# Remainder tokens of a recurrence-and-FFN kernel: from 128 partitions by batch to 96 partitions with two tokens of every batch

## The chip, the cores and the metric

The kernel runs on one core of a Trainium2 chip. Times are device microseconds. Before the change the median of three runs is 236.07 us (235.56 to 237.6). One further execution was profiled; all views of the trace are of that one.

## The reference

For a batch of 4 sequences of 6,336 tokens with 256 channels, a gated recurrence runs along the tokens, and a highway layer follows on every token:

```python
sig = 1.0 / (1.0 + np.exp(-f_logit))
f = lower_bound + (1.0 - lower_bound) * sig
i = 1.0 - f
for t in range(S):
    h = f[:, t] * h + i[:, t] * x[:, t]
    y[:, t] = h
H = np.maximum(y @ w_h, 0.0)
T = 1.0 / (1.0 + np.exp(-(y @ w_t + b_t)))
out = T * H + (1.0 - T) * y
```

Inputs and output are 32-bit floats in HBM, 26 MB each for `x`, `f_logit` and the output.

## The kernel before, in words

The 25,344 tokens are cut into 29 units (the table `UNITS`): mostly 1,024 tokens of one batch, some of 512 or 256 at both ends, and one, unit 15, of 768 tokens: the 192 tokens from 3,072 on of each of the four batches, which 1,024 does not divide. A row of the table holds the tokens per partition (k), the runs (batch, first token, count), the column at which the product e is split between VectorE and GpSimd, and how the tokens of a partition are grouped for the product B, for the output matmuls O and for the stores o.

Each unit goes through the same steps, which the code names by a letter:

- `l`, `x`: loads of `f_logit` and `x` by SyncE (L223). A partition takes k consecutive tokens. For one batch `in_dram` (L212) gives the access "p j d"; for unit 15 it gives "b p j d", so that the batch (4 steps) is the outer step, and partitions 32b to 32b+31 hold 6 tokens each of batch b.
- `U`: ScalarE's sigmoid of the negated logits (L259), giving u, the part that does not gate.
- `B`: the product bv = u * x (L281 on GpSimd; L279 on VectorE for units 0 and 1).
- `T`, `V`: TensorE's transposes of u and bv to channels by tokens (L287, L305), for each half h of the channels.
- `F`: ScalarE makes the gate f = 1 + ncc * u from the transposed u, and puts the tokens in order (L297).
- `S`: VectorE's scan along the tokens (L313), with the state carried per batch and half. Unit 15 has eight scans of 192.
- `Z`, `G`: the two matmuls of the layer (L324); `A`: ScalarE's sigmoid t (L335); `D`: VectorE's maximum d (L339); `E`, `P`: the product e = d * t on VectorE (L345) and, for the columns past the split, on GpSimd (L352).
- `O`: TensorE sums y and e back into token rows, in groups of two tokens per partition (L363, L364); `C`: ScalarE copies them out of PSUM (L376); `o`: SyncE stores them (L381).

The order of all the work is written out in one list, `OPS`. It is also the order in which each engine issues its own part, and it names the buffer of each result (`l15@l2` is the load of unit 15's logits into slot l2; there are four slots each for l and x, eight for o). All loads and stores stand in one queue, SyncE's: a load that waits for its slot, or a store that waits for its copy, holds everything behind it. The list was made by a planner outside the kernel. `X` items are matmuls on zeros.

In the list before, the part of SyncE around unit 15 reads: `l14 o6.0 x17 o7.0 o5.0 x14 l15 x15 o8.1 o4.0 o8.0 l16 o5.1 x16 o9.0 x18`, and later `o10.0 o15.1 o15.0 x24 l23 l26`.

Of the kernel before, what the change touches and what calls it, by code (L numbers as in the profile page):

```python
# [36 lines left out]
    (6, ((0, 3072, 192), (1, 3072, 192), (2, 3072, 192), (3, 3072, 192)), 384, (4, 2), (2, 2, 2), (4, 2), ()),  # L37
# [23 lines left out]
X4@s0 Tb@s0 cst l0@l0 x0@x0 W1 W0 U0.0@u0 B0.0@bv0 X1@s1 T0.0@s1 T0.1@s2 F0.1@f0 F0.0@f1 w1 l1@l1 U1.0@u1  # L61
V0.0@s3 V0.1@s0 dia v1 S0.0@y0 X7@s2 T1.0@s2 S0.1 w0 v0 l2@l2 x1@x1 F1.0@f2 U2.0@u2 T1.1@s1 X3@pp0 Z0.0@pp0
X1@s3 T2.0@s3 F1.1@f3 A0.0@t0 B1.0@bv1 V1.1@s2 S1.1@y1 T2.1@s0 G0.0@pp1 Z0.1@pp0 V1.0@s1 D0.0@d0 X1@pp1
G0.1@pp1 S1.0 F2.0@f1 F2.1@f0 A0.1 x2@x2 B2.0@bv2 l3@l3 l4@l0 U3.0@u0 x3@x3 l5@l1 B3.0@bv0 X1@pp0 Z1.1@pp0
D0.1 A1.1@t1 U4.0@u1 G1.1@pp1 D1.1@d1 V2.0@s3 T3.1@s2 T3.0@s0 Z1.0@pp0 G1.0@pp1 S2.0@y2 F3.1@f3 F3.0@f2
V2.1@s1 S2.1 X1@s3 T4.1@s3 T4.0@s2 F4.1@f1 A1.0 F4.0@f0 D1.0 E1@e0 E0@e1 X4@pp1 G2.0@pp1 D2.0@d1 x4@x0 x5@x1
l6@l2 U5.0@u2 V3.0@s0 Z2.1@pp0 V3.1@s1 O0.0@s3 Z2.0@pp1 S3.0@y3 S3.1 A2.1@t1 A2.0 T5.1@s2 T5.0@s0 G2.1@pp0
C0.0@o0 F5.1@f2 D2.1 B4.0@bv1 B5.1@bv2 B5.0 Z3.0@pp1 V4.0@s1 O1.0@s3 Z3.1@pp0 V4.1@s2 A3.0@t0 F5.0@f3 A3.1
U6.0@u0 G3.1@pp1 G3.0@pp0 C1.0@o1 S4.0@y4 S4.1 D3.1@d0 D3.0 E2@e1 E3@e0 x6@x2 l8@l3 l7@l0 x7@x3 x8@x0 o0.0
o1.0 l9@l1 x9@x1 Z4.0@pp1 V5.0@s1 T6.0@s0 S5.0@y0 A4.0@t1 F6.0@f0 B6.0@bv0 B6.1 Z4.1@pp0 A4.1 O2.0@s2 O3.1@s3  # L70
C3.1@o2 U8.0@u1 C2.0@o3 V5.1@s0 G4.1@pp1 T6.1@s3 G4.0@pp0 S5.1 D4.0@d1 D4.1 V6.0@s1 U7.0@u2 F6.1@f1 Z5.0@pp0
T8.1@s0 V6.1@s2 Z5.1@pp1 S6.0@y1 B7.1@bv1 B7.0 A5.0@t0 F8.1@f3 A5.1 O3.0@s3 G5.1@pp0 T7.1@s1 S6.1 D5.1@d0
T7.0@s0 G5.0@pp1 E4@e0 D5.0 F7.1@f2 C3.0 F7.0@f0 Z6.1@pp0 V7.0@s2 A6.1@t1 U9.0@u0 O2.1@s1 O4.1@s3 V7.1@s0
Z6.0@pp1 B8.0@bv2 B8.1 S7.0@y3 S7.1 E5@e1 A6.0 T8.0@s2 G6.1@pp0 G6.0@pp1 T9.0@s0 C2.1 C4.1@o4 F8.0@f1 F9.0@f0
O4.0@s1 V8.1@s3 O5.2@s2 C4.0 C5.2@o5 l13@l2 l10@l3 U10.0@u2 x10@x2 l11@l0 D6.0@d1 D6.1 B9.1@bv0 B9.0 S8.1@y2
E6@e0 G7.1@pp1 T9.1@s0 O5.1@s1 Z7.0@pp0 D7.1@d0 T10.1@s2 V8.0@s3 C5.1@o6 F9.1@f2 A7.0@t0 F10.1@f3 O5.0@s1 C5.0
U11.0@u1 V9.0@s0 G7.0@pp0 Z7.1@pp1 O6.1@s2 C6.1@o7 x11@x3 o3.0 l12@l1 l17@l3 x12@x0 x13@x1 o2.0 S8.0 B10.0@bv1
B10.1 B11.1@bv2 O5.3@s1 D7.0 T11.0@s3 V9.1@s2 A7.1 P7.0@e1 B11.0 Z8.1@pp0 F11.0@f1 C5.3 A8.1@t1 S9.0@y4 S9.1
Z8.0@pp1 O6.3@s3 O6.2@s1 A8.0 T10.0@s0 G8.1@pp0 G8.0@pp1 O6.0@s2 C6.3@o0 U13.0@u0 C6.2 C6.0 F10.0@f0 D8.1@d1
D8.0 E7 E8@e0 V10.1@s3 Z9.0@pp0 S10.1@y0 O7.3@s1 A9.0@t0 C7.3@o1 T11.1@s2 F11.1@f2 V10.0@s0 G9.1@pp1 O7.0@s1  # L80
C7.0@o2 D9.1@d0 U12.0@u2 Z9.1@pp0 O7.2@s3 C7.2 S10.0 V11.0@s2 G9.0@pp1 V11.1@s1 O7.1@s3 T13.0@s0 A9.1 C7.1
F13.0@f3 Z10.1@pp0 D9.0 P8.0 B13.0@bv0 B13.1 B12.1@bv1 P9.0@e1 B12.0 T12.0@s3 G10.0@pp1 O8.2@s0 A10.1@t1
Z10.0@pp0 F12.0@f0 C8.2@o3 A10.0 l14@l0 o6.0 x17@x2 o7.0 o5.0 x14@x3 l15@l2 O8.3@s3 C8.3 x15@x1 o8.1 o4.0
S11.0@y1 D10.0@d1 S11.1 O8.1@s2 O8.0@s0 C8.1@o7 C8.0 U14.0@u1 G10.1@pp1 T13.1@s3 G11.1@pp0 T12.1@s2 D10.1 E9
E10@e0 D11.1@d0 V12.0@s1 Z11.0@pp1 O9.3@s0 S12.0@y3 F12.1@f1 F13.1@f2 A11.0@t0 C9.3@o2 Z11.1@pp0 O9.0@s2
V12.1@s3 S12.1 C9.0@o6 A11.1 B14.1@bv2 P10.0 B14.0 U15.0@u0 V13.0@s0 O9.2@s1 C9.2 O9.1@s2 G11.0@pp1 C9.1
U17.0@u2 G12.0@pp0 T14.1@s3 V13.1@s1 o8.0 l16@l1 o5.1 x16@x0 o9.0 x18@x3 l19@l0 D11.0 D12.0@d1 B15.0@bv1
P11.0@e1 S13.1@y2 S13.0 E11 Z12.1@pp1 G12.1@pp0 F14.1@f0 T15.1@s2 T14.0@s3 O10.3@s1 A12.1@t1 Z12.0@pp1
F14.0@f1 C10.3@o3 V14.0@s3 O10.1@s1 O10.2@s0 A12.0 Z13.1@pp1 C10.1@o4 F15.1@f2 A13.1@t0 C10.2 O11.2@s1
O10.0@s2 D12.1 S14.0@y4 B17.1@bv0 B15.1 P12.0@e0 G13.1@pp0 D13.1@d0 C11.2@o7 C10.0 U16.0@u1 O11.3@s0 T15.0@s1  # L90
V14.1@s3 C11.3 O11.0@s2 F15.0@f3 C11.0@o5 Z13.0@pp1 G13.0@pp0 O11.1@s0 A13.0 B16.1@bv2 S14.1 D13.0 E12 E13@e1
P13.0 B16.0 B17.0 T16.0@s1 T17.1@s3 V15.0@s2 C11.1 F16.0@f1 F17.1@f0 o9.1 l18@l2 o7.1 o6.1 l24@l3 o11.1 l20@l1
x19@x1 o10.1 S15.0@y0 Z14.1@pp0 Z14.0@pp1 O12.3@s0 V15.1@s1 O12.0@s3 T17.0@s2 A14.1@t1 C12.3@o6 A14.0 S15.1
G14.1@pp0 O12.1@s0 G14.0@pp1 D14.1@d1 D14.0 O12.2@s1 C12.0@o2 U18.0@u0 C12.2 C12.1 F17.0@f3 G15.1@pp0 V16.0@s3
P14.0@e0 D15.1@d0 S16.0@y1 E14 Z15.1@pp1 O13.2@s1 C13.2@o1 T16.1@s0 F16.1@f2 O13.0@s2 Z15.0@pp0 V16.1@s1
C13.0@o0 A15.1@t0 A15.0 V17.0@s0 O14.0@s3 C14.0@o7 S16.1 G15.0@pp1 O13.3@s2 O14.2@s3 O13.1@s1 D15.0 U19.0@u2
C13.3 B18.0@bv1 B18.1 P15.0@e1 B19.1@bv2 S17.0@y3 C13.1 C14.2@o3 Z16.0@pp0 G16.0@pp1 A16.0@t1 T18.0@s2
V17.1@s1 T18.1@s3 O14.1@s0 D16.0@d1 S17.1 F18.0@f1 G16.1@pp0 Z16.1@pp1 F18.1@f2 C14.1 A16.1 V18.0@s2 T19.1@s3
T19.0@s0 O14.3@s1 F19.1@f3 C14.3 F19.0@f0 D16.1 E15 E16@e0 S18.0@y2 P16.0 B19.0 Z17.0@pp1 V18.1@s3 O15.1@s1
G17.1@pp0 O15.0@s0 o12.1 l22@l2 o13.0 o11.0 x20@x0 l21@l0 o12.0 o14.1 x23@x2 x22@x3 x21@x1 o10.0 D17.1@d0  # L100
S18.1 A17.0@t0 C15.1@o6 U20.0@u1 C15.0 G17.0@pp1 O16.0@s2 C16.0@o0 Z17.1@pp0 A17.1 D17.0 T20.1@s1 O16.2@s0
O15.2@s2 V19.0@s3 B20.0@bv0 B20.1 P17.0@e1 Z18.0@pp0 C16.2@o5 C15.2@o2 F20.1@f1 A18.0@t1 G18.0@pp1 O16.3@s0
C16.3 O16.1@s2 V19.1@s1 S19.0@y4 D18.0@d1 S19.1 E17 U21.0@u0 Z18.1@pp0 V20.1@s3 T20.0@s0 G18.1@pp1 A18.1 C16.1
F20.0@f2 Z19.0@pp0 D18.1 S20.1@y0 B21.1@bv1 B21.0 P18.0@e0 A19.0@t0 O17.0@s1 T21.1@s2 F21.1@f0 U22.0@u2
V20.0@s0 G19.0@pp1 D19.0@d0 S20.0 G19.1@pp0 C17.0@o3 T21.0@s2 O17.3@s3 C17.3@o4 Z19.1@pp1 F21.0@f3 T22.1@s1
O17.1@s3 O17.2@s2 V21.1@s0 A19.1 D19.1 E18 E19@e1 o15.1 o15.0 x24@x0 l23@l1 l26@l0 C17.2 o17.1 o16.1 o16.0
S21.1@y1 Z20.1@pp1 C17.1 F22.1@f1 V21.0@s2 O18.1@s3 Z20.0@pp0 A20.1@t1 C18.1@o2 A20.0 S21.0 U23.0@u1 B22.0@bv2
P19.0 G20.0@pp1 O18.0@s1 O18.2@s3 G20.1@pp0 T22.0@s0 O18.3@s2 C18.0 C18.2@o6 C18.3 B22.1 D20.0@d1 D20.1
O19.2@s1 G21.1@pp1 U24.0@u0 F22.0@f2 C19.2@o4 D21.1@d0 B23.1@bv0 P20.0@e0 B23.0 x25@x1 l25@l2 o14.0 x26@x3
l28@l1 o17.0 o18.1 o13.1 o18.0 l27@l3 T23.0@s3 V22.1@s2 Z21.0@pp0 G21.0@pp1 V22.0@s0 A21.0@t0 S22.1@y3 S22.0  # L110
F23.0@f0 T24.0@s1 O19.3@s2 Z21.1@pp0 F24.0@f3 O19.1@s3 O19.0@s1 T23.1@s0 D21.0 A21.1 G22.0@pp0 C19.0@o5 C19.3
C19.1 F23.1@f1 E20 V23.0@s1 O20.2@s2 C20.2@o0 T24.1@s3 F24.1@f2 E21@e1 D22.0@d1 Z22.0@pp1 Z22.1@pp0 V23.1@s0
S23.0@y2 S23.1 B24.0@bv1 P21.0 B24.1 A22.0@t1 A22.1 O20.0@s2 C20.0@o7 U25.0@u2 O20.3@s3 G22.1@pp1 O21.0@s1
O21.3@s2 C21.3@o3 C21.0@o6 C20.3 G23.1@pp0 D22.1 D23.1@d0 B25.1@bv2 B25.0 O20.1@s0 V24.1@s2 T25.0@s1 C20.1
U26.0@u1 G23.0@pp1 V24.0@s3 T25.1@s0 P22.0@e0 S24.1@y4 D23.0 S24.0 E22 Z23.0@pp0 O21.2@s2 F25.1@f0 F25.0@f1
Z23.1@pp1 C21.2 V25.0@s0 O21.1@s1 V25.1@s2 A23.0@t0 A23.1 B26.1@bv0 B26.0 P23.0@e1 S25.1@y0 Z24.0@pp0 C21.1
U27.0@u0 A24.0@t1 G24.1@pp1 T26.1@s3 O22.2@s1 T26.0@s2 C22.2@o1 F26.0@f2 F26.1@f3 D24.1@d1 S25.0 Z24.1@pp0
T27.0@s1 G24.0@pp1 O22.3@s2 O22.1@s3 O22.0@s0 A24.1 C22.3 C22.1@o2 C22.0 F27.0@f0 Z25.0@pp0 V26.1@s2 D24.0 E23
E24@e0 x28@x2 x27@x0 o19.1 o19.0 o20.1 o20.0 o21.0 o22.0 o21.1 O23.2@s3 O23.0@s0 O23.3@s1 G25.0@pp1 A25.0@t0
C23.2@o4 C23.3 C23.0@o5 o23.1 o22.1 O23.1@s3 T27.1@s1 V26.0@s0 U28.0@u2 Z25.1@pp0 F27.1@f1 C23.1 S26.1@y1  # L120
P24.0 B27.0@bv1 B28.0@bv2 D25.0@d0 S26.0 A25.1 T28.1@s2 G25.1@pp1 T28.0@s1 O24.3@s3 G26.0@pp0 D25.1 D26.0@d1
# [10 lines left out]
def kernel(  # L132
# [66 lines left out]

    def need(key, n):  # L200
        if key not in st[n]:
            k = UNITS[n][0]
            shape, dt = {
                "l": ([P, 8, D], FP32), "x": ([P, 8, D], FP32), "u": ([P, 8, D], FP16), "bv": ([P, 4, D, 2], BF16),
                "f0": ([P, 8 * P], FP16), "f1": ([P, 8 * P], FP16), "y": ([P, NH, 8 * P], BF16),
# [222 lines left out]
```

## Time and profile before

| | |
|---|---|
| median of the runs | 236.07 us |
| profiled execution, its own time | 238.39 us |
| its span | 236.6 us |
| granted TensorE clock, mean | 0.962 |
| busy: PE, DVE, ACT, POOL | 201.3, 197.5, 201.0, 151.2 us |
| moved by DMA | 78.68 MB, 333 GB/s over the span |
| loads of 1,024 KB: issue to landing, median | 15.8 us (l), 14.8 us (x) |
| loads of 768 KB (unit 15) | one of l, one of x |
| ACT waited for l | 16.1 us in 4 waits, longest 9.5 |
| POOL waited for x | 38.3 us in 9 waits, longest 16.1 |
| SyncE's queue waited for ACT's copies | 78.0 us in 26 waits, longest 7.8 |

The profile names engines PE (TensorE), DVE (VectorE), ACT (ScalarE), POOL (GpSimd) and SP (SyncE). The page cuts the span in 40 slices of 5.9 us and gives the busy share of each engine in tenths; slices are counted from 0. A busy-time line gives a stretch, and for each engine the busy microseconds and the number of instructions, then the granted clock, the mean busy share of the 16 DMA engines, and GB/s.

### The profile page before, as it was taken

The page shows a single profiled execution, that of the slowest core. Times are in us where ns is not written, and L with a number is a line of the kernel's source. Part 1 is how long each engine was busy: PE and PEld are TensorE (multiplying, and loading weights), DVE is VectorE, ACT ScalarE, POOL GpSimd, SP SyncE. Part 2 cuts the span into 40 slices and gives each one's busy share as a digit, 9 for nine tenths or more (in the row PEclk, how much of TensorE's full clock was granted, in tenths as well). Part 3 has the DMA queues.
Part 4 walks back from the last instruction along what each step waited for, and adds up shares of the span by engine and source line. Part 5 has one row for each costly group of instructions (what it writes and reads, how often), then busy time and mean ns, then how long its engine had stood idle before and what let it go on. Part 6 is the DMA issues. An engine that isn't in the chain of part 4 may idle for free.

```text
span 236.6 us, 4629 instructions
## 1 busy us (share of the span) xinstructions
PE 201.3 (85%) x1818; PEld 141.1 (60%) x1818; DVE 197.5 (83%) x163; ACT 201.0 (85%) x248; POOL 151.2 (64%) x80
## 2 busy tenths in 40 slices
PE   7779889899999980688986969999949999999991
PEld 3356556576677660366664756766636777686771
DVE  3488999999999990394996988999946999999970
ACT  5799999999999940959949879999667999998892
POOL 2066568579889680049698637919887299878400
PEclk9999999999999998589999999999976999999999
DMA  6999999999999999559999599989999949547286
GB/s 210 350 423 421 417 414 421 418 420 419 419 418 334 382 208 232 180 171 332 425 425 377 208 346 345 425 320 427 375 341 416 375 179 346 222 159 288 107 336 269
DMA packets 16221, 78.68 MB, mean 333 GB/s; under 512 B 1732, under 2 KB 2248, under 8 KB 10824
## 3 DMA queue, kind: packets, MB, share of 16 engines
q1 hardware_dynamic: 16192, 78.39, 86.8%
q8 instruction: 14, 0.23, 0.4%
q14 instruction: 7, 0.06, 0.1%
q10 hardware_dynamic: 8, 0.00, 0.0%
HBM read 52.43 MB, written 25.95 MB: 331 GB/s over the span
## 4 chain that ended last, share of the span: by engine, by line
DMA 34%; PE 33%; DVE 19%; issue 6%; SPq 2%; POOL 2%; ACT 1%; ACTq 0%; DVEq 0%; POOLq 0%
DMA out_dram<-o 25%; DVE y L313 11%; DMA l<-in_f_logit_dram 9%; PE gp L324 8%; PE zp L324 8%; DVE d L339 7%; PE op L364 5%; PE op L363 4%; PE bT L305 4%; PE uT L287 4%; SPq L223 2%; DVE e L345 2%; ACT o L376 1%; POOL e L352 1%; POOL bv L281 1%
## 5 line engine op out<-in xcount | busy, mean ns | idle before, releaser
L281 POOL TENSOR_TENSOR bv<-u,x 128x1024 bf16<-128x1024 f16 (+1 forms) x49 | 103.9, 2138 | 58.6 <-DMA x<-in_x_dram 38.3
L313 DVE TENSOR_TENSOR_SCAN y<-f,y,bT 128x1024 bf16<-128x1024 f16 (+3 forms) x56 | 103.8, 1878 | 13.6 <-ACT o L376 9.1
L339 DVE SCALAR_TENSOR_TENSOR d<-y,ncc,gp 128x1024 bf16<-128x1024 bf16 (+3 forms) x58 | 63.6, 1112 | 11.1 <-PE gp L324 6.4
L376 ACT COPY o<-op 128x512 f32<-128x512 f32 x99 | 59.0, 651 | 6.9 <-DMA out_dram<-o 4.9
L259 ACT ACTIVATE u<-l 128x2048 f16<-128x2048 f32 (+3 forms) x29 | 49.9, 1721 | 16.2 <-DMA l<-in_f_logit_dram 16.1
L335 ACT ACTIVATE t<-zp,bt 128x1024 bf16<-128x1024 f32 (+3 forms) x58 | 60.4, 1056 | 3.2 <-issue 1.7
L363 PE MATMUL op<-diag,y 128*128 128x128 f16 x396 | 56.8, 224 | 6.6 <-ACT o L376 5.5
L297 ACT ACTIVATE f<-uT,ncc 128x1024 f16<-128x1024 f16 (+3 forms) x58 | 59.3, 1050 | 3.0 <-PE uT L287 3.0
L324 PEld LDWEIGHTS <-w_sb 128*128 128x128 f16 x408 | 38.5, 100 | 35.5 <-issue 10.5
L364 PE MATMUL op<-ident_b,e 128*128 128x128 bf16 x396 | 56.8, 226 | 2.0 <-DVE e L345 1.1
L364 PEld LDWEIGHTS <-e 128*128 128x128 bf16 x396 | 49.7, 142 | 13.0 <-issue 9.1
L352 POOL TENSOR_TENSOR e<-d,t 128x1152 bf16<-128x1152 bf16 (+1 forms) x20 | 46.9, 2345 | 14.6 <-DVE e L345 9.3
L324 PE MATMUL gp<-y,w_sb 128*128 128x512 bf16 (+1 forms) x204 | 53.3, 382 | 1.7 <-ACT t L335 0.9
L324 PE MATMUL zp<-y,w_sb 128*128 128x512 bf16 (+1 forms) x204 | 53.1, 380 | 1.4 <-ACT t L335 0.5
L363 PEld LDWEIGHTS <-y 128*128 128x128 bf16 x396 | 51.3, 143 | 4.5
L305 PE MATMUL bT<-ident_f,bv 128*128 128x128 f32 x198 | 32.9, 284 | 10.5 <-ACT o L376 9.1
L287 PE MATMUL uT<-ident_h,u 128*128 128x128 f16 x396 | 31.4, 224 | 5.5 <-ACT o L376 1.8
L287 PEld LDWEIGHTS <-u 128*128 128x128 f16 x396 | 26.6, 101 | 14.9 <-issue 5.1
L305 PEld LDWEIGHTS bT<-ident_f,bv 128*128 128x128 f32 x198 | 23.4, 145 | 17.3 <-ACT o L376 9.8
L345 DVE TENSOR_TENSOR e<-d,t 128x896 bf16<-128x896 bf16 (+4 forms) x29 | 21.2, 752 | 1.7 <-PE op L364 1.0
L313 DVE TENSOR_TENSOR_SCAN y<-f,bT 128x1024 bf16<-128x1024 f16 (+2 forms) x8 | 12.5, 1604 | 0.0
L386 PE MATMUL zeros<-zeros 128*128 128x512 bf16 x23 | 8.3, 471 | 2.7 <-DVE zeros L174 1.2
(25 smaller groups left out, 11.8 us busy)
## 6 DMA issues: line engine op xcount, KB each, us to landing
out_dram<-o SPq DMA_DIRECT2D x48, 512.0 KB, 10.0
l<-in_f_logit_dram SPq DMA_DIRECT2D x21, 1024.0 KB, 15.8
x<-in_x_dram SPq DMA_DIRECT2D x21, 1024.0 KB, 14.8
l<-in_f_logit_dram SPq DMA_DIRECT2D x5, 512.0 KB, 10.6
x<-in_x_dram SPq DMA_DIRECT2D x5, 512.0 KB, 9.0
out_dram<-o SPq DMA_DIRECT2D x3, 256.0 KB, 13.2
l<-in_f_logit_dram SPq DMA_DIRECT2D x1, 768.0 KB
x<-in_x_dram SPq DMA_DIRECT2D x1, 768.0 KB
```

What stands on the lines that cost most here:

```text
L259: pin(nc.scalar.activation(need("u", n)[:, :k], st[n]["l"][:, :k], AF.Sigmoid, scale=-1.0))
L281: on_pool(pin(nc.gpsimd.tensor_mul(o, u, v)))
L287: pin(nc.tensor.transpose(t[:, j * P:(j + 1) * P], st[n]["u"][:, j, h * P:(h + 1) * P], ident_h))
L297: pin(nc.scalar.activation(a, b, AF.Identity, scale=ncc[:, h:h + 1], bias=1.0))
L305: pin(nc.tensor.transpose(w[:, g], v[:, g, h * P:(h + 1) * P, 0], ident_f))
L313: pin(nc.vector.tensor_tensor_scan(y[:, h, c:c + m], st[n][f"f{h}"][:, c:c + m], st[n]["bT", h][:, c:c + m], 0.0 if prev is None else prev ...
L324: pin(nc.tensor.matmul(p[:, a:e], w_sb[:, k, ki, m * P:(m + 1) * P], st[n]["y"][:, ki, a:e], start=ki == 0, stop=ki == NH - 1))
L335: pin(nc.scalar.activation(need("t", n)[:, m, :N], st[n]["zp", m][:, :N], AF.Sigmoid, bias=bt[:, m:m + 1]))
L339: pin(nc.vector.scalar_tensor_tensor(need("d", n)[:, m, :N], st[n]["y"][:, m, :N], ncc[:, m:m + 1], st[n]["gp", m][:, :N], op0=ALU.mult, o ...
L363: pin(nc.tensor.matmul(o, st[n]["y"][:, h, j:k * P:k], diag[:, h], start=True, stop=False))
L364: pin(nc.tensor.matmul(o, st[n]["e"][:, h, j:k * P:k], ident_b, start=False, stop=True))
L376: pin(nc.scalar.copy(st[n]["o", s][:, j0 - base:j1 - base].rearrange("p j d -> p (j d)"), st[n]["op", q][:, :(j1 - j0) * D]))
```

## The change

Unit 15 takes 96 partitions and 8 tokens in each: two consecutive tokens of each of the four batches. A copy of it between HBM and SBUF now has the partition as its outer step on both sides ("p b j d"), with pieces of two tokens (2,048 bytes). Its transposes, products and output matmuls are sized by 96 rows, and the tokens are put in order by batch in `F`, `V` and `O`. Its groups are those of the 1,024-token units: two products B of 4, four output groups of 2, two stores of 4 tokens per partition; the split of e is at column 448 instead of 384. The other units compute as before. The list `OPS` is made anew from end to end: the same items, but for unit 15's, in another order with other buffers, with 24 matmuls on zeros instead of 23.

```diff
-    (6, ((0, 3072, 192), (1, 3072, 192), (2, 3072, 192), (3, 3072, 192)), 384, (4, 2), (2, 2, 2), (4, 2), ()),
+    (8, ((0, 3072, 192), (1, 3072, 192), (2, 3072, 192), (3, 3072, 192)), 448, (4, 4), (2, 2, 2, 2), (4, 4), ()),
...
-    def in_dram(ap, n):
-        k, runs = UNITS[n][:2]
-        (b, a, m), q = runs[0], len(runs)
-        if q == 1:
-            return ap[b, a:a + m, :].rearrange("(p j) d -> p j d", j=k)
-        assert [(r, a, m) for r in range(b, b + q)] == list(runs)
-        return ap[b:b + q, a:a + m, :].rearrange("b (p j) d -> b p j d", j=k)
+    def shape(n):
+        k, runs = UNITS[n][:2]
+        r = len(runs)
+        b, a, m = runs[0]
+        assert [(b + i, a, m) for i in range(r)] == list(runs) and m * r % k == 0
+        return m * r // k, k, r, k // r, m * r
+
+    def copy(n, tile_, dram, to_dram=False, j0=0, j1=None):
+        np_, k, r, kr, _ = shape(n)
+        j1 = k if j1 is None else j1
+        b, a, m = UNITS[n][1][0]
+        t = tile_[:np_, :j1 - j0]
+        if r == 1:
+            d = dram[b, a:a + m, :].rearrange("(p j) d -> p j d", j=kr)[:, j0:j1]
+        else:
+            d = dram[b + j0 // kr:b + j1 // kr, a:a + m, :].rearrange("b (p j) d -> p b j d", j=kr)
+            t = t.rearrange("p (b j) d -> p b j d", j=kr)
+        pin(nc.sync.dma_start(d, t) if to_dram else nc.sync.dma_start(t, d))
...
-            pin(nc.tensor.transpose(t[:, j * P:(j + 1) * P], st[n]["u"][:, j, h * P:(h + 1) * P], ident_h))
+            pin(nc.tensor.transpose(t[:, j * np_:(j + 1) * np_], st[n]["u"][:np_, j, h * P:(h + 1) * P], ident_h[:np_, :np_]))
...
+            a = f[:, :N].rearrange("c (b p j) -> c b p j", b=r, j=kr)
+            b = st[n]["uT", h][:, :N].rearrange("c (b j p) -> c b p j", b=r, j=kr)
...
+            b, i = divmod(j, kr)
+            cols = slice(b * np_ * kr + i, (b + 1) * np_ * kr, kr)
...
-                pin(nc.tensor.matmul(o, st[n]["y"][:, h, j:k * P:k], diag[:, h], start=True, stop=False))
+                pin(nc.tensor.matmul(o, st[n]["y"][:, h, cols], diag[:, h], start=True, stop=False))
```

The first lines of the two lists, and SyncE's order around unit 15:

```diff
-X4@s0 Tb@s0 cst l0@l0 x0@x0 W1 W0 U0.0@u0 B0.0@bv0 X1@s1 T0.0@s1 T0.1@s2 F0.1@f0 F0.0@f1 w1 l1@l1 U1.0@u1
-V0.0@s3 V0.1@s0 dia v1 S0.0@y0 X7@s2 T1.0@s2 S0.1 w0 v0 l2@l2 x1@x1 F1.0@f2 U2.0@u2 T1.1@s1 X3@pp0 Z0.0@pp0
+l1@l0 X4@s0 Tb@s0 l0@l1 cst dia U1@u0 x0@x0 U0@u1 X3@s1 T0.1@s1 T1.0@s2 T0.0@s3 F0.1@f0 F0.0@f1 F1.0@f2
+B0.0@bv0 V0.1@s0 S0.1@y0 V0.0@s1 S0.0 W1 W0 w0 w1 v0 v1 X8@pp0 Z0.0@pp0 l2@l2 x1@x1 U2@u2 A0.0@t0 Z0.1@pp1
...
-l14 o6.0 x17 o7.0 o5.0 x14 l15 x15 o8.1 o4.0 o8.0 l16 o5.1 x16 o9.0 x18
+l16 o3.0 o6.1 x16 o7.1 o5.1 l15 x15 x17 o6.0 x19 o9.0 o9.1 l18 o7.0 o10.0 l19
...
-x21 o10.0 o15.1 o15.0 x24 l23 l26
+x23 o15.0 l23 o16.0 x24 l25 o16.1 x25 o17.1 l27 o18.0 x28 o14.0 l26 o18.1 o15.1
```

## The prediction

> **What bounds the kernel now.** I read the page's slices first, to see where all engines stop; then busy time by stretch, which separates the undisturbed part from the disturbed one; then the timelines of ScalarE and SyncE at the worst place; then the landing times of the stores issued there.
>
> ```profile
> PE 201.3 (85%) x1818; PEld 141.1 (60%) x1818; DVE 197.5 (83%) x163; ACT 201.0 (85%) x248; POOL 151.2 (64%) x80
> PE   7779889899999980688986969999949999999991
> DVE  3488999999999990394996988999946999999970
> ACT  5799999999999940959949879999667999998892
> GB/s 210 350 423 421 417 414 421 418 420 419 419 418 334 382 208 232 180 171 332 425 425 377 208 346 345 425 320 427 375 341 416 375 179 346 222 159 288 107 336 269
> ```
>
> One slice is 5.9 us. Two engines, ACT and DVE, are each busy about 200 of 236.6 us, and both are full until slice 13. At slice 15 (89 to 95 us) every engine stands at 0 or near it, while the moved bytes fall from 420 to about 200 GB/s over four slices. A second, smaller hole is at slices 29 and 30.
>
> The busy time by stretch (busy us of each engine, granted clock, share of the 16 DMA engines, GB/s):
>
> ```profile
> 12.00:84.00 72.00, 65.51 (x597) 45.45 (x595) 69.85 (x57) 71.29 (x84) 54.74 (x26) 1.00 1.00 405
> 24.00:84.00 60.00, 55.20 (x508) 38.50 (x506) 59.65 (x43) 60.00 (x68) 46.38 (x23) 1.00 0.99 402
> 84.00:108.00 24.00, 13.70 (x99) 8.91 (x99) 13.52 (x9) 11.75 (x13) 7.88 (x4) 0.79 0.77 210
> 100.00:104.00 4.00, 4.00 (x30) 2.63 (x28) 4.00 (x4) 2.35 (x3) 0.32 (x1) 0.68 0.25 104
> 84.00:192.00 108.00, 87.51 (x790) 62.38 (x791) 85.64 (x63) 84.23 (x99) 68.07 (x32) 0.92 0.91 329
> 192.00:228.00 36.00, 35.72 (x350) 26.50 (x349) 35.48 (x29) 33.86 (x48) 26.77 (x13) 1.00 0.58 224
> ```
>
> From 24 to 84 us ACT (fourth engine column) never stops and DVE (third) stops for 0.35 us: there the two compute engines bound the kernel, with the DMA just keeping up. From 84 to 192 DVE stands for 22.4 us and ACT for 23.8. The line for 100 to 104 us shows what kind of hold it is: the DMA share is 0.25 and 104 GB/s move, a quarter of 420. A quarter of 16 engines is four, and unit 15's transfers are the only ones whose outer step counts four (the batches).
>
> What ACT and the SyncE queue did there:
>
> ```profile
> 84.19 1.30 ACT L335 ACTIVATE t<-zp,bt 128x1024 bf16<-128x1024 f32 x1
> 94.97 1.48 ACT L259 ACTIVATE u<-l 128x1536 f16<-128x1536 f32 x1 [9.48 <-DMA l<-in_f_logit_dram]
> ```
> ```profile
> 74.44 1.15 SPq L223 DMA_DIRECT2D l<-in_f_logit_dram  x1
> 75.70 0.58 SPq L223 DMA_DIRECT2D x<-in_x_dram  x1
> 77.73 3.24 SPq L381 DMA_DIRECT2D out_dram<-o  x3
> ```
>
> The 128x1536 activation is unit 15's sigmoid; it waits 9.48 us for the load issued at 74.44. Of stores issued from 77.5 to 87 us, and from 40 to 75, the landing times are:
>
> ```profile
> DMA to landing us min/median/max: 26.9/27.7/28.4
> ```
> ```profile
> DMA to landing us min/median/max: 4.9/7.5/17.3
> ```
>
> Ordinary stores behind unit 15's two loads land 27.7 us after issue, where 7.5 was the median before: every transfer needs all engines, so each waits for the four clogged ones.
>
> **The change, part by part.**
>
> *Loads of unit 15.* Each is 768 x 1,024 B = 0.786 MB. Both at the shown 104 GB/s need 15.1 us; at the 420 GB/s of slices 2 to 11 they need 3.7. Now the outer step is 96 rows, of four pieces of 2,048 B each. No row shows 96; the nearest are the 128-row transfers at 420 GB/s, and the four-row ones at 104. So the two cost 3.7 to 15.1 us of the stream; 96 is near 128, so I take 3.7.
>
> *Stores of unit 15.* 0.786 MB together: 7.6 us on four engines, 1.9 on all. Behind these stores (issued around 152 us) stand the loads of units 23, 24 and 26, and the hole at slices 29 and 30 follows.
>
> [...]
>
> *Compute of unit 15*, from the rows by shape. ACT: the sigmoid becomes 2,048 long (1,973 ns for 1,482, +0.5) and there is one more eviction of 128x512 (651 ns, +0.65): +1.1 us. DVE: the product e takes 896 columns (767 ns for 551): +0.2; the eight scans of 192 stay (582 ns). POOL: the second bv product grows from 512 to 1,024 (2,158 for 1,170 ns), e shrinks by a sixth: +0.7, hidden, since POOL is 24% idle from 12 to 84 us. PE: 8 more matmuls in the output step, 4 and 2 more transposes, 14 in all at some 0.06 to 0.11 us spacing: about 1 us, hidden in PE's 9% idle there. ACT and DVE have no cover. That operations on 96 partitions cost the same by length is assumed; their cost lies between the same and three quarters of it.
>
> *The new list.* All issue orders change, with the same operations (one more zeros matmul, 24 for 23, about 0.2 us of PE's idle start). Head: S0 now stands ahead of the weight folds v0 and v1, for which DVE waited 1.70 us; l0 stands behind l1, 256 KB, some 0.9 us at the 283 GB/s of the first 12 us. So between -1.7 and +0.9. I take 0, because DVE's next product waits for x1 anyway (till 10.52 us), and the same bytes stand ahead of x1 as before. Tail: the last units are the same; the 228 to 236.6 stretch keeps its cost, within about 1 us. Middle: in the new order of SyncE, 25 loads stand directly behind a store, 18 before; l15 itself is behind two stores, the first of which waits for C7.3. From C7.3 to U15 ACT has about 14 us of work and a 1 MB load lands a median 15.8 us after issue, so a wait of about 2 us can arise there.
>
> *The sum.* In 84 to 192 us DVE has 85.64 us of work, plus 0.2. At the undisturbed rate of 12 to 84 (69.85 of 72, 97.0%) that takes 88.5 us instead of 108: 19.5 saved. By ACT: 84.23 + 1.1 at 71.29 of 72 takes 86.2: 21.8 saved. The engine that ends later decides: 19.5. This leaves about 2.7 us for stalls of the new order, which covers the possible 2 us at U15. PE ran at a granted clock of 0.50 around 96 to 102 us, after the standstill; that goes with it. The span becomes 236.6 - 19.5 = 217.1. The profiled execution took 238.39, 1.8 around its span; so 218.9. It stands 2.3 above the median of the runs (236.07), so the median is predicted at 216.6. The DMA's floor is lower: 78.4 MB at 420 GB/s are 187 us. What is late next is nothing single: ACT and DVE are both full.
>
> Bounds: with no stall at all DVE saves 22.4 - 0.2 = 22.2, the median is 213.9, and a head 1 us better gives 213. If only the first hole is filled: 24 us with 13.52 of work at 97% are 13.9, +0.2, so 9.9 saved, 226.2. The likeliest case's own range is 213 to 220.5.
>
> **Rivals.**
>
> *Only the first hole goes (226).* The standing time of 108 to 192 us (DVE 11.9, ACT 11.5) then belongs to the queue order, not to unit 15: SyncE waits 78 us in all for evictions ahead of its stores, with loads behind them. For it: DMA share is at 1.0 in much of that stretch. Against: there the loads start from empty buffers after 20 us of hold, and the second hole follows unit 15's stores.
>
> *The transfers stay on few engines (236).* If the outer step that counts is still the batch, both holes stay, moved in time. Against: the partition is now outermost on both sides of the copy.
>
> *Slower: loads held behind stores (240).* Place: SyncE's single queue, from l15 on. Price: apart from unit 15's waits of 16.1 and 9.5 us, five late loads from 84 to 192 us cost POOL and ACT 22.6 - 16.1 + 14.9 - 9.5 = 11.9 us, 2.4 each. The seven further loads behind stores, all late, cost 16.8 and still leave 2.7 saved; it decides from the ninth late load on ((19.5 + 2.4) / 2.4), and ten give 236.1 - 19.5 + 24 = 240.6. Against: from 24 to 84 us the same kind of queue cost ACT nothing.
>
> **How the numbers follow.** About 1% is what a measurement of this kernel can tell from no change. Chances: the forecast 0.70, only the first hole 0.17, below 213 by a better head or tail 0.03 (these three are faster: 0.90), transfers unchanged 0.04 (same), held loads 0.06 (slower). The range 213 to 227 holds the forecast and the first rival and leaves out 0.13.
>
> **What would show it.** Right: no slice with all engines near 0; slices 14 to 17 at 400 GB/s or more; no stretch at DMA share 0.25 with about 104 GB/s; stores issued near unit 15's loads landing within 17 us; ACT's wait for l near 0 to 3 us instead of 14.9; ACT busy about 202 and DVE about 198 of some 217 us; PE's clock at 1.0 through the middle. Wrong: a DMA share of 0.25 again (transfers not spread); idle ACT and DVE of over 5 us in the second half without such a stretch (queue order); or busy sums that grow by more than 3 us (operations on 96 rows or 2 KB pieces dearer than taken).

## The result, and the profile after

The changed kernel takes 215.35 us (median of 4 runs, 213.65 to 215.8); the kernel before, with one more run beside it, 236.45. The ratio is 0.909, with a 95% interval of 0.903 to 0.916. The prediction was 216.6, within 213 to 227. The profiled execution took 215.32 us, with a span of 213.5 (before: 238.39 and 236.6). The one before was 2.3 us slower than its median and the one after was at its median, so the spans differ by 23.1 us and the medians by 21.1. Of all executions below, one of the last experiment is left out of its ratio, since it ran at a granted clock of 0.846 and took 226.06 us.

The page of the changed kernel, the same lines as shown of before; a slice is now 5.3 us:

```profile
PE 194.2 (91%) x1803; PEld 139.3 (65%) x1833; DVE 194.6 (91%) x163; ACT 200.5 (94%) x249; POOL 152.0 (71%) x80
PE   6777987987999999999999999999999999999991
DVE  2647999999999999999999999999999999999970
ACT  5669999999999999999999999999999999998982
GB/s 188 403 417 424 414 421 424 413 414 424 414 424 423 415 419 283 205 338 416 427 415 425 422 415 420 421 421 429 416 386 420 361 350 407 237 103 98 295 297 295
```

From slice 4 to slice 35 ACT and DVE stand at 9 throughout and PE is never below 7. ACT's busy time is what it was (200.5 for 201.0), so nearly all of the 23.1 us that the span lost is idle time of ACT: 35.6 us before, 13.0 now. One thing stays: the moved bytes still dip, at slices 15 to 17 (80 to 96 us), and neither ACT nor DVE shows it.

Busy time by stretch of the changed kernel (columns as before: PE, weight loads, DVE, ACT, POOL, clock, DMA share, GB/s):

```profile
12.00:84.00 72.00, 63.44 (x576) 44.44 (x584) 68.44 (x55) 70.77 (x83) 54.12 (x26) 1.00 1.02 413
24.00:84.00 60.00, 53.71 (x490) 37.90 (x498) 59.53 (x43) 59.99 (x67) 47.57 (x23) 1.00 1.02 411
84.00:108.00 24.00, 23.32 (x241) 17.63 (x243) 23.70 (x21) 24.00 (x31) 20.78 (x10) 1.00 1.03 343
84.00:192.00 108.00, 105.54 (x1037) 78.94 (x1053) 107.19 (x80) 107.61 (x133) 87.82 (x41) 1.00 0.96 370
```

From 84 to 192 us DVE works 107.19 of 108 us and ACT 107.61; before it was 85.64 and 84.23. The granted clock is 1.00 throughout. Unit 15's sigmoid follows its neighbours without a wait (ACT's timeline of the changed kernel: start, duration, instruction; an idle time before it would stand in brackets):

```profile
89.19 1.25 ACT L385 COPY o<-op 128x512 f32<-128x512 f32 x2
90.13 1.95 ACT L264 ACTIVATE u<-l 96x2048 f16<-96x2048 f32 x1
91.94 1.11 ACT L385 COPY o<-op 128x512 f32<-128x512 f32 x2
```

### The profile page after: what moved, and what is told of

Its sections match the earlier page's. It is cut to its first block, busy times and chain, and to the rows that moved or that the text cites. A ratio compares the mean times of both kernels' runs of the same rounds, so it can differ in the third digit from the quotient of the medians.

```text
span 213.5 us, 4633 instructions
## 1 busy us (share of the span) xinstructions
PE 194.2 (91%) x1803; PEld 139.3 (65%) x1833; DVE 194.6 (91%) x163; ACT 200.5 (94%) x249; POOL 152.0 (71%) x80
## 4 chain that ended last, share of the span: by engine, by line
ACT 39%; PE 32%; issue 10%; DVE 8%; POOL 2%; ACTq 0%; DVEq 0%; POOLq 0%
ACT o L385 11%; ACT f L304 11%; ACT t L342 11%; PE zp L331 8%; PE gp L331 7%; ACT u L264 6%; DVE y L320 5%; PE bT L313 4%; PE op L372 4%; PE uT L291 4%; PE op L371 4%; DVE d L346 3%; POOL bv L285 2%; PE zeros L394 1%; DVE e L352 0%
## 5 line engine op out<-in xcount | busy, mean ns | idle before, releaser
L285 POOL TENSOR_TENSOR bv<-u,x 128x1024 bf16<-128x1024 f16 (+1 forms) x49 | 104.6, 2162 | 34.2 <-DVE e L352 13.0
L385 ACT COPY o<-op 128x512 f32<-128x512 f32 (+1 forms) x100 | 62.1, 706 | 0.7 <-PE op L372 0.7
L371 PE MATMUL op<-diag,y 128*128 128x128 f16 (+1 forms) x400 | 56.7, 224 | 1.0 <-ACT o L385 0.4
L372 PE MATMUL op<-ident_b,e 128*128 128x128 bf16 (+1 forms) x400 | 56.9, 225 | 0.6 <-DVE e L352 0.6
L371 PEld LDWEIGHTS <-y 128*128 128x128 bf16 (+1 forms) x400 | 51.4, 142 | 5.4 <-DVE y L320 0.5
L372 PEld LDWEIGHTS <-e 128*128 128x128 bf16 (+1 forms) x400 | 50.1, 142 | 5.4 <-issue 1.5
L313 PE MATMUL bT<-ident_f,bv 128*128 128x128 f32 (+1 forms) x200 | 31.0, 276 | 2.0 <-DVE bv L283 1.2
L291 PEld LDWEIGHTS <-u 128*128 128x128 f16 (+1 forms) x400 | 25.7, 98 | 10.0 <-ACT u L264 3.4
L291 PE MATMUL uT<-ident_h,u 128*128 128x128 f16 (+1 forms) x400 | 30.0, 220 | 2.4 <-ACT u L264 1.4
L313 PEld LDWEIGHTS bT<-ident_f,bv 128*128 128x128 f32 (+1 forms) x200 | 22.6, 142 | 6.9 <-DVE bv L283 1.4
L352 DVE TENSOR_TENSOR e<-d,t 128x896 bf16<-128x896 bf16 (+3 forms) x29 | 18.7, 657 | 0.4 <-ACT t L342 0.4
## 6 DMA issues: line engine op xcount, KB each, us to landing
l<-in_f_logit_dram SPq DMA_DIRECT2D x1, 768.0 KB, 11.9
```

The lines of the kernel that those rows point to most:

```text
L285: on_pool(pin(nc.gpsimd.tensor_mul(o, u, v)))
L291: pin(nc.tensor.transpose(t[:, j * np_:(j + 1) * np_], st[n]["u"][:np_, j, h * P:(h + 1) * P], ident_h[:np_, :np_]))
L313: pin(nc.tensor.transpose(w[:, i // 2::kr // 2], v[:np_, g, h * P:(h + 1) * P, 0], ident_f[:np_, :np_]))
L371: pin(nc.tensor.matmul(o, st[n]["y"][:, h, cols], diag[:, h], start=True, stop=False))
L372: pin(nc.tensor.matmul(o, st[n]["e"][:, h, cols], ident_b, start=False, stop=True))
L385: pin(nc.scalar.copy(st[n]["o", s][:np_, j0 - base:j1 - base].rearrange("p j d -> p (j d)"), st[n]["op", q][:np_, :(j1 - j0) * D]))
```

## The experiments

**The old layout with the new list.** Is it the list? Edit: the table's row of unit 15 and all functions as before the change; the new list, without the two items of the fourth output group.

> The kernel before (unit 15 on 128 partitions, its transfers with the batch as outer step) with the new list, without the fourth output group of unit 15, which it does not have. If the four-engine transfers are what cost the time: the holes come back under the new list, a stretch at DMA share 0.25 with about 104 GB/s, 230 to 240 us. If the new list is what gained: 214 to 219 us, ACT and DVE idle little in the middle.

Measured: 231.06 us (230.81 to 231.34), ratio to before 0.975 (0.970 to 0.979). The holes are back. Stretches of its trace:

```profile
84.00:192.00 108.00, 95.28 (x890) 69.82 (x889) 95.30 (x69) 93.25 (x111) 75.16 (x36) 0.95 0.92 333
96.00:98.00 2.00, 0.00 (x0) 0.00 (x0) 0.00 (x0) 1.60 (x2) 0.00 (x0) 0.91 0.25 101
```

A quarter of the DMA share with 101 GB/s: the four engines alone, under the new list too. With the old layout the new list is 5.65 us faster than the old one (in the medians of the runs side by side), but it does not take the holes away.

**The new layout with the old list.** Edit: the changed code with the list of before, and

```diff
- C15.2@o2
+ C15.2@o2 O15.3@s2 C15.3
```

> The changed code (96 partitions) with the old list, to which the fourth output group of unit 15 and its copy are added next to the third. If the transfers are what cost the time: 214 to 220 us. If the new list gained: 230 us or more. If the old list has waits of its own behind the first hole: about 226 us, with 5 us or more of ACT's idle time from 108 to 192 us.

Measured: 217.48 us (217.21 to 217.97), ratio 0.918 (0.913 to 0.923). So the code alone, with the list that was made for the other layout, brings 19.2 of the gain, and the new list some 2 on top. In its trace ACT is busy for 104.09 us from 84 to 192, DVE for 102.83: about 4 us of ACT's idle time belong to the old list there, not the 11.5 that the first rival gave it. One of them is a wait of unit 15's sigmoid for its load, 0.99 us, which the changed kernel does not have.

**The old kernel with its transfers split by batch.** Is it the layout, or the number of engines? Edit in the kernel before (the store likewise):

```diff
-        pin(nc.sync.dma_start(need(key, n)[:, :k], in_dram(src, n)))
+        t = need(key, n)
+        if len(UNITS[n][1]) == 1:
+            pin(nc.sync.dma_start(t[:, :k], in_dram(src, n)))
+        else:
+            for b, a, m in UNITS[n][1]:
+                pin(nc.sync.dma_start(t[32 * b:32 * b + 32, :k], src[b, a:a + m, :].rearrange("(p j) d -> p j d", j=k)))
```

> The kernel before, old list, old layout; each transfer of unit 15 becomes four, one for each batch, with 32 partitions as outer step. Nothing else changes. If the number of engines is what counts: no stretch at DMA share 0.25, 214 to 220 us, as with 96 partitions. If the layout itself (pieces, 96 rows) or the new list is needed: 230 us or more.

Measured: 219.40 us (218.63 to 221.03), ratio 0.927 (0.920 to 0.933). The tokens lie where they lay, the list is the old one, only the outer step of a transfer is 32 instead of 4: 17.3 us of the gain come with that. So the cause is the outer step of the transfer, not the place of the tokens. That it acts by the number of DMA engines, the packets in the trace of the kernel before show: from 100 to 104 us a mean of 4.1 are in flight, from 40 to 60 us 16.2, and a 4 KB packet takes a median of 159 ns in both. So four engines are not slow; they have a backlog. Of the sixteen signals of completion of a store issued at 77.73 us, behind unit 15's loads, twelve came from 80.9 to 82.3 us and four from 103.0 to 104.7. Four engines were still behind at 133 us, and again at 192, after unit 15's stores (a DMA share of 0.26 in both). Stretches of the kernel before:

```profile
133.00:136.00 3.00, 3.00 (x29) 2.05 (x28) 3.00 (x3) 2.12 (x3) 1.64 (x1) 1.00 0.26 100
192.00:195.00 3.00, 3.00 (x34) 2.46 (x33) 3.00 (x3) 3.00 (x5) 3.00 (x3) 1.00 0.26 107
```

**The same, for the loads alone.** The stores of unit 15 stay on four engines.

> As the one split by batch, but for the loads of unit 15 alone; its two stores stay on four engines. If the second hole (168 to 180 us in the kernel before, 4.4 us of DVE) comes from the stores: 3 to 6 us slower than with both split, and a hole of DVE some 15 to 30 us after these stores. If the second hole only follows from the first: the same as with both split, within 1 us.

Measured: 220.02 us (219.27 to 220.78), ratio 0.928 (0.923 to 0.933), against 0.927 (0.920 to 0.933) with both split: not told apart, where 3 to 6 us were expected. The hole itself is there. The same stretch, with the loads alone split and then with both:

```profile
140.00:160.00 20.00, 17.34 (x168) 12.30 (x166) 18.46 (x13) 18.18 (x22) 15.23 (x8) 1.00 0.96 378
```
```profile
140.00:160.00 20.00, 19.09 (x175) 13.27 (x174) 20.00 (x15) 20.00 (x24) 15.73 (x8) 1.00 0.94 347
```

and its end in ACT's timeline, of the kernel with the loads alone split:

```profile
153.50 1.30 ACT L340 ACTIVATE t<-zp,bt 128x1024 bf16<-128x1024 f32 x1
156.63 1.91 ACT L264 ACTIVATE u<-l 128x2048 f16<-128x2048 f32 x1 [1.82 <-DMA l<-in_f_logit_dram]
```

A load behind the four-engine stores comes 1.82 us late. At the same place ACT waited 3.61 us in the kernel before, and with both split it does not wait. DVE's side of the hole is the wait before one product d; here it is in the kernel before, and with the loads alone split:

```profile
178.57 1.28 DVE L339 SCALAR_TENSOR_TENSOR d<-y,ncc,gp 128x1024 bf16<-128x1024 bf16 x1 [4.27 <-issue]
```
```profile
160.96 1.28 DVE L344 SCALAR_TENSOR_TENSOR d<-y,ncc,gp 128x1024 bf16<-128x1024 bf16 x1 [2.50 <-POOL bv L286]
```

With both split DVE runs its products d there without a wait. So the stores on four engines make a hole of 2.50 us of DVE and 1.82 of ACT by themselves, somewhat over half of the second hole of the kernel before; the rest was an after-effect of the first. What of it reaches the end is less than these runs can tell.

**Why the bytes dip while unit 15 is loaded.** In the changed kernel slices 15 to 17 fall to 283, 205 and 338 GB/s, where the prediction had 400 or more. Five kernels change where unit 15's loads come from or how they are cut; the first changes its stores in the same way.

*Batch by batch*, four transfers of 96 rows of 2 KB, stores likewise:

```diff
-            d = dram[b + j0 // kr:b + j1 // kr, a:a + m, :].rearrange("b (p j) d -> p b j d", j=kr)
-            t = t.rearrange("p (b j) d -> p b j d", j=kr)
+            for i in range(j0 // kr, j1 // kr):
+                d = dram[b + i, a:a + m, :].rearrange("(p j) d -> p j d", j=kr)
+                ti = t[:, i * kr - j0:(i + 1) * kr - j0]
+                pin(nc.sync.dma_start(d, ti) if to_dram else nc.sync.dma_start(ti, d))
+            return
```

> The changed kernel; each transfer of unit 15 is made batch by batch (96 partitions, pieces of 2 KB; loads four at a time, stores two). In the changed kernel the rate fell to 200 to 280 GB/s from 80 to 96 us, while unit 15 was loaded. If the jumps between the batches within one transfer slow the reads: the rate stays at 400 GB/s or more in this stretch. If it is the 2 KB pieces, or something at this time or place: the dip stays. The time is 213 to 216 us either way, since ACT did not wait there.

Measured: 214.56 us (213.39 to 215.31), ratio 0.902 (0.895 to 0.908).

*Near pieces*: for the loads, the first batch alone.

```diff
+                d = dram[0, a:a + m * r, :].rearrange("(b p j) d -> p b j d", b=r, j=kr)
```

> The changed kernel, but unit 15 is loaded from 768 consecutive tokens of the first batch, in the same pieces of 2 KB and the same order of partitions, with 192 tokens (192 KB) between the four pieces of a partition instead of a whole batch (6.2 MB). It thus computes unit 15 from other tokens. If the distance of a whole batch slows the reads: no dip at 80 to 96 us. If the pieces or their order do: the dip stays at 200 to 280 GB/s.

*Other rows* (`a = 0` for the loads):

> The changed kernel, but unit 15 is loaded from the first 192 tokens of each batch instead of tokens 3072 to 3263, in the same pieces and order, so it computes unit 15 from other tokens. If the place in HBM makes the reads of unit 15 slow: no dip of the rate at 80 to 96 us. If the shape of the transfer does: the dip to 200 to 300 GB/s stays, as with near pieces. Time 213 to 216 us either way.

*One run*: 8 KB in one piece for each of the 96 partitions.

```diff
+                d = dram[0, a:a + m * r, :].rearrange("(p j) d -> p j d", j=k)
```

> The changed kernel, but unit 15 is loaded from 768 consecutive tokens of the first batch from token 3072 on, 8 KB in one piece for each of the 96 partitions, so it computes unit 15 from other tokens. If pieces of 2 KB, or the jumps between them, slow the reads: no dip. If 96 partitions, the moment or the place do: the dip stays. Time 213 to 216 us either way.

*128 rows*:

```diff
+                t = tile_[:, :k]
+                d = dram[0, a:a + P * k, :].rearrange("(p j) d -> p j d", j=k)
```

> The changed kernel, but unit 15 is loaded as an ordinary unit is: 128 partitions, 8 KB in one piece for each, 1,024 consecutive tokens of the first batch from token 3072 on (1 MB instead of 0.75; only the first 96 partitions are used, so unit 15 is computed from other tokens). If transfers to 96 partitions are what slows the reads: no dip, 400 GB/s or more in every slice from 6 to 28. If the moment or the work beside it does: the dip at 80 to 96 us stays. Time 213 to 216 us either way.

The stretch from 82 to 92 us, in this order: the changed kernel, batch by batch, near pieces, other rows, one run, 128 rows.

```profile
82.00:92.00 10.00, 9.61 (x92) 6.95 (x92) 10.00 (x7) 10.00 (x13) 8.93 (x5) 1.00 1.07 224
```
```profile
82.00:92.00 10.00, 9.62 (x101) 7.44 (x100) 10.00 (x8) 10.00 (x14) 8.91 (x4) 1.00 1.01 284
```
```profile
82.00:92.00 10.00, 9.60 (x101) 7.53 (x102) 10.00 (x9) 10.00 (x13) 8.41 (x4) 1.00 1.06 222
```
```profile
82.00:92.00 10.00, 9.67 (x97) 7.19 (x95) 10.00 (x7) 10.00 (x13) 8.93 (x5) 1.00 1.06 235
```
```profile
82.00:92.00 10.00, 9.65 (x96) 7.06 (x95) 10.00 (x7) 10.00 (x12) 8.93 (x5) 1.00 1.04 240
```
```profile
82.00:92.00 10.00, 9.65 (x103) 7.45 (x102) 10.00 (x9) 10.00 (x13) 8.38 (x5) 1.00 1.01 397
```

The last two differ in the rows, 96 or 128 of the same 8 KB pieces (and so in the bytes, a third more with 128), and the rate is 240 or 397 GB/s. Near pieces, other rows and one run left the rate at 222 to 240. So the place in HBM, the distance between the pieces and their size don't make the dip; it goes with 96 rows instead of 128 in the loads. The packets say the same: in these 10 us an 8 KB packet took a median of 580 ns with 96 rows in one run and 313 ns with 128, while the DMA share was 1.04 and 1.01. All engines were busy and about half as fast, unlike the four of the kernel before, which were as fast as ever and alone. Each of these is one profiled execution, and not all are of the same chip.

The expectation of 400 GB/s in every slice from 6 to 28 was missed with 128 rows too, at slices 15 (363 GB/s) and 26 (398), so a remainder of the dip may have other causes. Cutting by batch makes it shallower (284), and why it does was not tried. In every one of the six ACT and DVE, third and fourth of the engine columns, are busy for 10.00 of 10 us: the dip costs no time here. That was close: in the changed kernel l15, issued at 77.57 us, landed 11.9 us later, 0.7 us before its sigmoid began. One execution each took 214.79 (near pieces), 214.83 (other rows), 215.05 (one run) and 213.62 us (128 rows).

The stores of unit 15 read 96 partitions and show no such dip: the first, issued at 136.9 us in the changed kernel, falls into slices 26 and 27, with 421 and 429 GB/s; around the second, from 165 to 168 us, the stream moved 382. Their 2 KB packets took a median of 84 ns, those of unit 15's loads 161 ns.

**Both again, on one chip.**

> The changed kernel again, for a comparison on one chip with the loads made batch by batch: 213.5 to 216 us.

> The changed kernel with unit 15's transfers made batch by batch, again. The dip of the rate was shallower with it (371 for 343 GB/s from 84 to 108 us), but ACT waits there in neither. If ACT and DVE alone set the time: within 1 us of the changed kernel. If the spared DMA time counts: 1 to 2 us faster.

Measured: 214.93 us, ratio 0.907 (0.904 to 0.911), and 214.41 us, ratio 0.905 (0.901 to 0.910). Not told apart: the spared DMA time does not show, as one expects where ACT and DVE are full. No run points to a version that is clearly faster than the changed kernel.

## Why the prediction was right, and where it was off

- *What bounds the kernel.* Right. The quarter DMA share was the four engines: with the outer step at 96 it is gone under either list, with 32 under the old one (the only one tried), and with 4 it is there under either list.
- *Loads of unit 15, 3.7 of 3.7 to 15.1 us.* This term was mis-sized. "96 is near 128, so I take 3.7" does not hold: from 82 to 92 us the stream moved 224 GB/s, so some 10 x (420 - 224) / 420 = 4.7 us of it were lost, and the two loads cost about 8.4 (an estimate; over the whole of slices 15 to 17 the loss is some 0.8 us more). The expected 400 GB/s in slices 14 to 17 was wrong for the same reason. It did not reach the sum, since the loads had been issued early enough: l15 landed 11.9 us after issue and 0.7 us ahead of its sigmoid, and ACT waited for no load in the stretch. Under the old list the same load cost a wait of 0.99 us. So the new list spared the sum, where the prediction had put a risk of about 2 us at U15.
- *Rows or size.* The term came from a row of 128-row transfers, which could not speak to 96: 240 GB/s with 96 rows against 397 with 128. That pair does not tell the rows from the size, since its transfers are 768 KB and 1 MB. But the size does not look like the cause here: cut to 192 KB, batch by batch, the loads ran at 284 GB/s rather than 224, and the first store of unit 15, 384 KB, ran within a stream of 421 and 429.
- *Stores of unit 15.* The mechanism is there, the size not: a hole of 2.5 us of DVE (1.8 of ACT) when they alone stay on four engines, 4.3 (3.6) in the kernel before, and no time that could be told apart at the end.
- *Compute of unit 15.* The sigmoid took 1,954 ns (1,973 taken; 2,057 on 128 rows in the same trace), four copies of 96x512 694 ns each (copies of 128x512: 706), bv on 96 rows 2,160 ns (on 128: 2,162), the scans 593 ns. That 96 partitions cost by length alone was right to within about 5% for these. PE's added work made no wait that could be seen.
- *The sum.* Predicted span 217.1, measured 213.5; the median 216.6 and 215.35. The predicted ratio, 0.918 to the 236.07 from which the sum started and 0.916 to the runs shown, lies at the upper edge of the measured interval. In DVE's terms: it stood idle for 39.1 us of the span before and for 18.9 after, so 20.2 us of idle time went where the prediction had 19.7 (22.4 less 2.7). The other 3.1 us of the miss are work: DVE's busy time shrank by 2.9 us (197.5 to 194.6), where it was to grow by 0.2.
- *How much of the agreement was luck.* The stretch from 84 to 192 us ran at 99.3% of DVE's time, not at the 97.0% of 12 to 84: the 2.7 us left for stalls were not needed, and the wait of 2 us that was thought possible at U15 did not come (ACT's waits in the stretch are 0.4 us in all). Under the old list the same stretch ran at 95.2% (102.83 of 108). So the rate was a fair middle, but nothing in the prediction said on which side of it the new list would fall. Against that gain, DVE had done 73.05 us of work by 84 us instead of 74.59, where the head was taken at no change; why is open. And the loads' missing 4.7 us met a list that had issued them early enough.
- *DVE's shorter work.* Of the 2.9 us, its products e give 2.5. Those on 128x896 took a mean of 617 ns after 767 before, but that mean hides two kinds. Before, 17 of the 19 took 593 to 626 ns; the two others took 2,258 and 1,924 ns. Each of these two began while a GpSimd product ran, and ended 0.48 us after it. The first of them (the first of the two e in this row) and the GpSimd product beside it:

```profile
114.96 2.79 DVE L345 TENSOR_TENSOR e<-d,t 128x896 bf16<-128x896 bf16 x2
114.60 2.15 POOL L281 TENSOR_TENSOR bv<-u,x 128x1024 bf16<-128x1024 f16 x1 [0.84 <-DMA x<-in_x_dram]
```

  Two undisturbed ones take less than half of that:

```profile
186.39 1.15 DVE L345 TENSOR_TENSOR e<-d,t 128x896 bf16<-128x896 bf16 x2
```

  In the traces of the kernel before, the changed one and the first four experiments, all ten such e that began over 0.1 us before the end of a GpSimd product ended 0.48 to 0.49 us after it, the longest after 2,459 ns (old layout, new list). So this product waited for GpSimd's in all ten. The prediction took the mean of 767 ns as the cost of 896 columns, and so could not see that two meetings with GpSimd, of some 1.6 and 1.3 us, stood in it. That the stalls bring the two together fits the longest ones, which are in the kernels with transfers on four engines, but no run tried it.
- *The rival of the first hole alone (226).* Refuted: with the old list and spread transfers 217.5 and 219.4 us. Of the 11.5 us that ACT stood from 108 to 192, 2.9 (84 - 81.08) are left under the old list with the new layout. The four engines had still been behind at 133 us, in the middle of that stretch.
- *The rival of held loads (240).* SyncE's queue now waits 90.7 us for copies, more than the 78.0 before, and 25 loads stand behind stores. ACT waits for a load for 0.4 us in the whole run. The long wait of the queue cost ACT nothing, since the loads behind it still landed before it needed them; GpSimd, which has time to spare, waited 10.5 us for x. A slip in this rival: (19.5 + 2.4) / 2.4 is 9.1, so by its own numbers the tenth late load decides, not the ninth.
- *The rival of unchanged transfers.* Refuted by the 0.25 that is gone.

## What to carry to other kernels

Read the outer step of every DMA. Here a step of 4 left twelve of sixteen engines without work for stretches of time, and what was queued behind, on all engines, landed late (stores 27.7 us after issue in the median, 7.5 before that); the DMA share of 0.25 named the number. Splitting the transfer, or putting the partition outermost, brought 17.3 and 19.2 of the 21.1 us with the old order of work, and the new order alone brought 5.65.

Do not take a size between two measured ones for the nearer of them: loads to 96 rows kept all engines busy (a DMA share of 1.04 to 1.07) and still moved little more than half of what loads to 128 did (222 to 240 GB/s for 397). Here that cost nothing, because ACT and DVE stayed full and the load had been issued just early enough. And do not take a mean as the cost of one operation before seeing its spread: a mean of 767 ns was 17 times 0.6 us and twice some 2 us, and the two were waits.

## What the runs showed of the hardware that was not expected

- While loads to 96 partitions run, the whole stream is slow: 222 to 240 GB/s from 82 to 92 us with each load in one transfer of 96 rows (284 cut by batch), against 397 with 128. An 8 KB packet took 580 ns against 313, with all engines busy. Stores from 96 partitions showed no such dip (421 and 429 GB/s during the first, 382 around the second; 84 ns for a packet of 2 KB, 161 in the loads).
- The four engines that held unit 15's transfers worked at their usual pace (159 ns for a 4 KB packet, from 40 to 60 us and from 100 to 104); only the other twelve had nothing to do (a DMA share of 0.25 from 100 to 104 us).
- With loads to 32 partitions at a time the stream was slow as well: 263 GB/s from 76 to 86 us in the kernel split by batch, with ACT busy for all of it. No run of its own separates the 32 rows from what else moved there:

```profile
76.00:86.00 10.00, 9.81 (x102) 7.38 (x101) 9.94 (x7) 10.00 (x13) 7.61 (x5) 1.00 1.02 263
```

- VectorE's product e (bf16, 128x896) waited while a GpSimd product ran: ten of ten that began over 0.1 us before one's end, in six traces, ended 0.48 to 0.49 us after it.
- TensorE's granted clock fell during the standstill before the change: PE was idle from 87.9 to 97.0 us, and the clock was 1.00 from 88 to 92, 0.54 from 92 to 96, 0.50 from 96 to 102 and 0.86 from 102 to 104. In the changed kernel, without the standstill, it was 1.00 from 84 to 192.
